# Four frequency groups of a spectral block: products summed on GpSimd and transposed by DMA, and the join's other TensorE work moved to other steps

## The chip, the cores and the metric

The kernel runs on one core of one Trainium2 chip. The metric is the device time of one launch in microseconds (us). A core has TensorE (PE; its weight loads are shown as PEld), VectorE (DVE), ScalarE (ACT), GpSimd (POOL) and SyncE (SP, which here issues nearly all DMAs). Each engine works through its own instructions in program order and waits on semaphores.

## The reference

One transformer block with adaptive layer norm, on x of 2048 x 640 (bf16): a global spectral filter (a 2-D real FFT over tokens and channels, a product with a complex weight, the inverse FFT), then a gated feed-forward of width 1728.

```python
mod = (_silu(c) @ w_mod).reshape(c.shape[0], 6, 1, -1)
sa, ca, ga, sb, cb, gb = (mod[:, i] for i in range(6))
h = _layernorm(x) * (1 + ca) + sa
X = jnp.fft.rfft2(h.astype(jnp.float32), axes=(-2, -1)) * (w_r + 1j * w_i)
x = x + ga * jnp.fft.irfft2(X, s=(S, D), axes=(-2, -1)).astype(jnp.bfloat16)
h = _layernorm(x) * (1 + cb) + sb
x = x + gb * ((_silu(h @ w_gate) * (h @ w_up)) @ w_down)
```

## The kernel before, in words

It is one long program in five stages. The order of each engine's instructions is the order of the Python calls; nothing is reordered afterwards.

1. **Forward transform** (to about 33 us): layer norm of x, a DFT over tokens and channels as matmuls, result in `A_sb`, for 81 of the channel frequencies l (the rest follow by symmetry).
2. **Join** (about 33 to 61 us; lines 515 to 812), where the change lies. The 81 frequencies are cut into 21 groups of mostly four (`groups`, `NG = 21`; group 4 holds l = 0 and 80, group 5 three). A loop over steps g = 0 to 21 works as a hand-written pipeline. For group g + 2, `stage_a`: `mix` (four PE matmuls, L581, out of transposed blocks `B2` that four DMA transposes and four PE transposes made) into one of two PSUM bank pairs, then `prod` (two DVE products with the weight table `Wt`, L605) into the SBUF tile `PPs[g]`, one of four slots, where the frequency index is the innermost. For group g, `stage_b`: eight PE matmuls with the identity (L613) that at once add the two halves of the complex product and transpose it, and an ACT copy to `Y2` (L616). For pairs of groups, some steps later, `stage_c`: PE matmuls with the inverse table (L643), and `evac`, an ACT copy of two banks (L652) to `Em` (l below 64) or `Er`.
   Into these steps other work is laid: the gate vector `ga_mod` (L713, steps 1 and 2), the weight table's mirrored columns `turn` (L381, ACT copies L387) and `wsum` (POOL, L424), a special path for frequency 0 over tokens (`sp_w`, `sp_gather`, `sp_mm`, `sp_ev`; steps 3, 5, 9, 11, 13), whose last step copies two rows to SBUF and has SP move them by DMA to partition 127 (L707, L708), and the modulation columns `mod_col` (L594). Already there, and unused, is `presum`: with a group in the set `PRE` (empty), POOL would add the halves and PE would only transpose.
   The pairs' `stage_c` comes at the step of their last group + 2.
3. **Inverse transform over channels** (about 61 to 80 us): 16 token tiles t; `s1em`, `s1er` (L729, L738), then L1266 and L1269, and a DVE sum with x (L1271). After t = 1 the second layer norm of the first two tiles runs; at t = 4 SP issues its DMA transpose (`ln2_tr`, L871), POOL scales the result (`ln2_mod`, L879), and at t = 15 PE begins the feed-forward with it (`gu13`, L1083).
4. **Feed-forward of the first two tiles** (L1095, L973) and 5. **of the other 14 tiles** (L996, L1125), PE without a pause to the end.

SP's queue in the join, in order: four DMA transposes `t2_dma` (L541), the tables `Htab` (L551) and `RI` (L552), two 800 KB pieces of `w_mod` (L553, L554; the second is used in step 20 only), the two rows of the special path (L707, L708, after ACT's copy L706), `B_w_down` (L815 to L819), `Wp13` (L822, L823), three loads of gate and up weights (L827), the transpose of stage 3 (L871), and the last two loads of up weights (L827). `presum` and its place in the loop are these lines:

```python
if 1 < g < NG - 2 and g + 2 in PRE:
    presum(g + 2)
...
for u, gs in enumerate(units):
    if gs[-1] + (1 if gs[0] >= NG - 2 else 2) == g:
        stage_c(u)
        evac(u)
```

Of the kernel before, what the change touches and what calls it, by code (L numbers as in the profile page):

```python
# [11 lines left out]
BF16 = mybir.dt.bfloat16  # L12
# [3 lines left out]
ALU = mybir.AluOpType  # L16

S, D, FF = 2048, 640, 1728
NT, P = 16, 128
# [147 lines left out]
def adaln_block_kernel(ctx, tc, A_x, A_w_r, A_w_i, B_x, B_w_gate, B_w_up, B_w_down, c, w_mod, out):  # L167
# [165 lines left out]
    if True:  # L333
# [41 lines left out]
        def turn(lo, i, b=3, eng=None):  # L375
            hi = lo + 16
            lo = max(lo, 1)
            n = hi - lo
            ps = psum[:, b, 0:32 * n].rearrange("p (a k c l) -> p a k c l", a=2, k=8, c=2)
            for a in range(2):  # L380
                nc.tensor.matmul(ps[:, a], lhsT=flipb[:], rhs=_rev(Wraw, 2568 * i + (161 - hi if a else lo), [[321, 8], [160, 2], [1, n]]),  # L381
                                 start=True, stop=True)
            if b < 4:
# [50 lines left out]
        def sp_w():  # L434
            tp = psum[0:81, 4, 192:256].bitcast(BF16).rearrange("p (v h a k) -> p v h a k", v=2, h=2, a=2)
# [98 lines left out]
    if True:  # L534
# [18 lines left out]
        nc.sync.dma_start(wm_r[:, :, 2, :], wm_m[:, :, 2, :])  # L553
        nc.sync.dma_start(wm_r[:, :, 3, :], wm_m[:, :, 3, :])  # L554
        Wd_sb = rA.cut(0, [NFC, D])
# [41 lines left out]
        def prod(g, xps, hl, v0=0, v1=3):  # L597
            ls = groups[g]
            n = len(ls)
            if g not in PPs:  # L600
                PPs[g] = rM.cut(1536 * (g % 4), [3, 2, NT, 2, n])
            xv = xps[:, :n, 0:192].rearrange("p i (v h k m) -> p v h k m i", v=3, h=2, k=NT)
            st = ls[1] - ls[0]
            in1 = _rev(Wt, (160 - ls[0] if hl else ls[0]) + WP * v0, [[WP, v1 - v0], [321, NT], [160, 2], [-st if hl else st, n]])
            nc.vector.tensor_tensor(PPs[g][:, v0:v1, hl], xv[:, v0:v1, hl], in1, ALU.mult)  # L605

        def stage_b(g, PP):
            n = len(groups[g])
            yps = banks((g + 1) % 2, 1, [4, 128])
            Q = Qs.pop(g, None)  # L610
            for ps in (1, 0) if Q is None else (0,):
                for i in range(n):
                    nc.tensor.matmul(yps[:, i, :], lhsT=_rev(PP if Q is None else Q, 64 * n * ps + i, [[n, 128]]), rhs=identb[:],  # L613
                                     start=(i == 0 and (ps == 1 or Q is not None)), stop=(ps == 0 and i == n - 1))
            Y2 = rY.cut(4096 if g == 4 else 1024 * (g % 4), [4, 128])
# [29 lines left out]
        def evac(u):  # L645
# [5 lines left out]
            else:  # L651
                (nc.vector.tensor_copy if g == NG - 6 else nc.scalar.copy)(  # L652
                    ep_views(l0 // 4 * 4, 8), banks(4 if g == NG - 4 else 6, 2, [8, 128])[0:127].rearrange("p i q -> p q i"))
# [8 lines left out]

        def gap(parts, i, w, b):
            return psum[0:parts, b + i // 2, 192 + 256 * (i % 2):192 + 256 * (i % 2) + w]

        def sp_mm(i, g):
            b = 2 + 2 * (g % 2)
            if i == 3:
# [22 lines left out]
        def sp_ev(i, g):  # L691
            b = 2 + 2 * (g % 2)
            if i == 3:
# [48 lines left out]

        PPs, Y2s, Qs = {}, {}, {}
        PRE = set()
        SPG = (9, 11, 13, 5)
        t2_pe(0)
# [11 lines left out]
        turn(32, 1, 7, act)  # L758
        wsum(32, 48, 8, nc.gpsimd)
        for rk in (0, 8):  # L760
# [3 lines left out]
        for g in range(NG + 1):  # L764
            if g == 9:
                nc.gpsimd.tensor_copy(sgnc[:], Kstab[:, 576:577])
            if g == 6:
                sp_gather()
            if 1 < g < NG - 2:
                if g in SPG:  # L770
                    sp_mm(SPG.index(g), g)
                if g == 3:
                    tp = sp_w()
                stage_a(g + 2)
                if g == 3:
                    sp_wc(tp)
                if g in SPG:
# [3 lines left out]
            if g in (4, 9):  # L781
                wsum(64, 80, 8 * (g // 9), nc.gpsimd)
            if g in (11, 12):
                h4 = slice(4 * (g - 11), 4 * (g - 11) + 4)
                nc.gpsimd.tensor_scalar(sgn_H[:, h4, 1], sgn_H[:, h4, 0], sgnc[:, 0:1], 1.0, ALU.mult, ALU.mult)
            if g == NG - 3:
                nc.vector.tensor_copy(modcols[:, 2, :], psum[:, 2, 192:197])
                nc.vector.tensor_scalar_add(one_p_cb[:], psum[:, 4, 192:197], 1.0)
            if g in (14, 16):
                i = (16 - g) // 2  # L790
# [7 lines left out]
            if g == 6:  # L798
# [605 lines left out]
```

## Time and profile before

| what | value |
|---|---|
| time, median of 3 runs | 249.57 us (247.81 to 250.02) |
| the profiled execution | 248.34 us, of which the span of its instructions is 246.3 us |
| busy over the span | PE 97%, PEld 76%, DVE 83%, ACT 69%, POOL 29% |
| granted TensorE clock | 1.00 |
| `stage_b` matmuls L613 | eight in 0.45 us |
| `prod` L605 (128 x 384) | mean 549 ns, one every 0.47 us back to back |
| ACT copy L616, ACT copy L652 | mean 598 ns, 1026 ns |
| DMA transpose of the first two tiles (L871) | issued at 70.39 us, landed 7.03 us later |

How to read it: times inside the execution count from the first instruction. A busy PE is near the bound only where it has no gaps; what a change in one stage is worth depends on which wait ends last there, and the chain of waits that ended last is the view for that. "Landing" of a DMA is the time from its issue until its semaphore says that all data are there.

### The profile page before, as it was taken

What the parts mean: (1) busy time and instruction counts of PE and PEld (TensorE: products, weight loads), DVE (VectorE), ACT (ScalarE), POOL (GpSimd) and SP (SyncE); (2) the same over time, 40 slices, a digit from 0 to 9 for tenths busy, and PEclk for the clock granted to TensorE, in tenths of its full rate; (3) what the DMA queues carried; (4) which work ended last, traced back from release to release, by engine and by line L of the source; (5) the groups of instructions that cost most, each with busy time, mean ns of one, the idle gap of its engine ahead of it and who ended that gap; (6) DMA issues with size and microseconds to landing.
All of it is one profiled execution on the core that took longest, in us unless ns stands there. A gap on an engine that the chain in (4) does not pass through costs nothing.

```text
span 246.3 us, 6008 instructions
## 1 busy us (share of the span) xinstructions
PE 239.1 (97%) x2262; PEld 187.8 (76%) x2262; DVE 203.4 (83%) x479; ACT 171.2 (69%) x343; POOL 70.9 (29%) x116
## 2 busy tenths in 40 slices
PE   8889999999999999999999999999999999999994
PEld 2678889999998887788887778887765666656773
DVE  4798777897499996989989968788998777789964
ACT  4789887998988797588864588765247777773220
POOL 4368896660424523002004400001422000004400
PEclk9999999999999999999999999999999999999999
DMA  6999979969999999500005110202411000000111
GB/s 204 381 339 290 342 179 179 253 234 293 289 374 266 194 266 190 123 3 1 3 0 106 59 53 3 53 0 43 86 38 53 0 1 3 0 0 4 53 53 53
DMA packets 44142, 31.19 MB, mean 127 GB/s; under 512 B 21873, under 2 KB 41810, under 8 KB 44114
## 3 DMA queue, kind: packets, MB, share of 16 engines
q1 hardware_dynamic: 42176, 26.15, 39.8%
q0 software_dynamic: 1376, 4.26, 7.5%
q10 hardware_dynamic: 562, 0.41, 0.6%
q8 instruction: 17, 0.28, 0.5%
q14 instruction: 11, 0.09, 0.1%
HBM read 23.49 MB, written 2.62 MB: 106 GB/s over the span
## 4 chain that ended last, share of the span: by engine, by line
PE 84%; DMA 5%; DVE 4%; POOL 2%; ACT 2%; issue 1%; ACTq 0%; DVEq 0%; POOLq 0%
PE psum L1125 36%; PE psum L996 19%; PE psum L1095 6%; PE psum L613 4%; PE psum L973 3%; DMA rW<-rL 3%; PE psum L581 3%; PE psum L404 2%; DMA rX<-in_A_x_dram 2%; PE psum L643 2%; PE psum L1083 2%; DVE bn6a L337 2%; PE psum L729 1%; ACT rE L407 1%; DVE rE L369 1%; POOL rW L879 1%
## 5 line engine op out<-in xcount | busy, mean ns | idle before, releaser
L1125 PEld LDWEIGHTS <-rW 128*128 128x128 bf16 (+1 forms) x429 | 41.9, 98 | 12.6
L1125 PE MATMUL psum<-rW 128*128 128x256 bf16 (+1 forms) x247 | 42.2, 287 | 0.0
L1022 POOL TENSOR_TENSOR rM<-rM,rL 128x320 f32<-128x320 f32 x6 | 5.5, 909 | 97.1 <-ACT rL L1021 97.1
L996 PEld LDWEIGHTS <-rE 128*128 128x128 f16 (+1 forms) x196 | 18.9, 97 | 8.0 <-DVE rE L950 0.3
L605 DVE TENSOR_TENSOR rM<-psum,rW 128x384 bf16<-128x384 f32 (+2 forms) x42 | 20.5, 543 | 4.0 <-PE psum L581 2.7
L996 PE MATMUL psum<-rE 128*128 128x320 f16 (+1 forms) x147 | 22.9, 299 | 0.0
L1163 ACT COPY rX<-psum 128x384 f32<-128x384 f32 (+2 forms) x27 | 14.0, 519 | 7.4 <-PE psum L1125 7.3
L1156 ACT COPY rH<-psum 128x384 f32<-128x384 f32 (+2 forms) x27 | 14.0, 517 | 7.2 <-PE psum L1125 6.5
L1125 PEld LDWEIGHTS <-rE 128*128 128x128 f16 x156 | 15.3, 98 | 4.7
L1160 DVE TENSOR_TENSOR rH<-psum,rM 128x512 bf16<-128x512 f32 (+1 forms) x24 | 15.0, 624 | 4.1 <-PE psum L1125 2.2
L1179 ACT ACTIVATE rL<-psum 128x384 bf16<-128x384 f32 (+2 forms) x27 | 14.4, 533 | 5.4 <-PE psum L1125 3.4
L1164 DVE TENSOR_TENSOR rX<-psum,rX 128x384 f32<-128x384 f32 (+2 forms) x27 | 16.3, 604 | 1.6 <-ACT rX L1163 1.4
L1150 ACT COPY rM<-psum 128x384 f32<-128x384 f32 (+2 forms) x27 | 13.9, 516 | 4.0 <-PE psum L1125 3.9
L1271 DVE SCALAR_TENSOR_TENSOR rM<-psum,rX 128x640 f32<-128x640 f32 x16 | 13.1, 821 | 3.9 <-ACT rL L733 2.4
L1125 PE MATMUL psum<-rW,rE 128*128 128x256 bf16 (+1 forms) x78 | 15.6, 290 | 0.0
L1125 PE MATMUL psum<-rE,rY 128*128 128x256 f16 (+1 forms) x78 | 15.6, 290 | 0.0
L1180 ACT ACTIVATE rL<-rX 128x384 bf16<-128x384 f32 (+2 forms) x27 | 15.1, 558 | 0.0
L337 DVE BATCH_NORM_STATS2 bn6a<-rX 128x6 f32<-128x320 bf16 x30 | 13.1, 480 | 2.4 <-DMA rX<-in_A_x_dram 2.4
L1095 PE MATMUL psum<-rW 128*128 128x256 bf16 x130 | 14.4, 273 | 0.0
L965 DVE TENSOR_TENSOR rA<-psum,rM 128x320 bf16<-128x320 f32 (+1 forms) x27 | 12.1, 472 | 2.4 <-PE psum L973 2.3
L424 POOL TENSOR_TENSOR rW<-rW 128x256 bf16<-128x256 bf16 x20 | 13.5, 704 | 1.4 <-DMA rW<-in_A_w_r_dram 0.7
L1095 PEld LDWEIGHTS <-rW 128*128 128x128 bf16 x130 | 12.7, 98 | 1.5
(231 smaller groups left out, 633.0 us busy)
## 6 DMA issues: line engine op xcount, KB each, us to landing
rM<-in_w_mod_dram SPq DMA_DIRECT2D x4, 800.0 KB, 8.1
out_dram<-rA SPq DMA_DIRECT2D x31, 80.0 KB, 1.6
rX<-in_A_x_dram SPq DMA_DIRECT2D x6, 320.0 KB, 6.3
rA<-in_B_w_down_dram SPq DMA_DIRECT2D x2, 960.0 KB, 6.3
rY<-in_B_w_gate_dram POOLq DMA_DIRECT2D x2, 832.0 KB, 7.8
rW<-in_B_w_gate_dram SPq DMA_DIRECT2D x1, 1440.0 KB, 10.0
rW<-in_A_w_i_dram SPq DMA_DIRECT2D x2, 642.0 KB, 11.1
rW<-in_A_w_r_dram SPq DMA_DIRECT2D x2, 642.0 KB, 10.5
```

What stands on the lines that cost most here:

```text
L337: nc.vector.bn_stats(bn6a[:, i % 2, k, :], x_sb[:, i, 320 * k:320 * k + 320])
L605: nc.vector.tensor_tensor(PPs[g][:, v0:v1, hl], xv[:, v0:v1, hl], in1, ALU.mult)
L996: nc.tensor.matmul(o, lhsT=lhs[rows(k), k], rhs=rhs[rows(k), k], start=start and k == ks[0], stop=stop and k == ks[-1], skip_group_check=True)
L1095: nc.tensor.matmul(gu[u], lhsT=Wgu[:, u, c5, ff * 128:(ff + 1) * 128], rhs=h2T[:, :, c5, :], start=(c5 == 0), stop=(c5 == NC5 - 1))
L1125: nc.tensor.matmul(o[:, f], lhsT=w, rhs=b, start=(start and f == 0 and i == 0), stop=(stop and f == len(groups[g]) - 1 and i == len(ops) - ...
L1150: nc.scalar.copy(c0, X)
L1156: nc.scalar.copy(c2, X)
L1160: nc.vector.tensor_tensor(c11, Z, c0, ALU.add)
L1163: nc.scalar.copy(c3, X)
L1164: nc.vector.tensor_tensor(c22, Y, c3, ALU.add)
L1179: nc.scalar.activation(g21, X, ACT.Silu, scale=-1.0)
L1180: nc.scalar.activation(g22, c22, ACT.Silu, scale=-1.0)
```

## The change

- Groups 7, 8, 11 and 12 are now in `PRE`. Their products are stored with the frequency outermost, POOL adds the halves (`presum`, 512 columns each, in steps 5, 6, 9, 10) into `Qd`, and after each second one SP issues a DMA transpose of 128 x 1024 into `Yd`, which `stage_c` uses directly. Their `stage_b` is gone: 32 PE matmuls with their weight loads, four ACT copies.
- `stage_c` of the pairs has a table of steps, `CAT`: (5,6) at step 7 instead of 8, (7,8) at 14 instead of 10, (9,10) at 11 instead of 12, (11,12) at 20 instead of 14, (17,18) at 19 instead of 20.
- `ga_mod` goes to steps 11 and 12, `turn(64)` to steps 7 and 8 (into the PSUM banks that `stage_b` leaves free), the special path to steps 5, 11, 13, 15 (its transposes `sp_w` to step 2), the columns `mod_col` from steps 16 to 18 to 7, 9, 14, 16, 18.
- The load of `w_mod`'s last piece goes from before the join to step 10, in SP's queue behind the second new transpose.
- Small moves: `sp_gather` from step 6 to 7, one `wsum` to step 2 and one from step 9 to 10; the evacuation that DVE does is now of pair (17,18).

```diff
-        nc.sync.dma_start(wm_r[:, :, 3, :], wm_m[:, :, 3, :])
...
-                    for c5 in {NG - 3: (0, 1), NG - 2: range(NC5), NG - 1: (2, 3, 4)}.get(g, ()):
-                        mod_col(psum[:, 2 + 2 * (g % 2), 192 + c5:193 + c5], wm_r[:, :, 1 + g % 2], c5)
+                    for c5 in {9: (0, 1, 2), 11: (3, 4), 16: (0, 1), 18: (2, 3), 20: (4,)}.get(g, ()):
+                        mod_col(psum[:, 2 + 2 * (g % 2), 192 + c5:193 + c5], wm_r[:, :, 2 - g % 2], c5)
...
-                PPs[g] = rM.cut(1536 * (g % 4), [3, 2, NT, 2, n])
+                PPs[g] = (rM.cut(1536 * (g % 4), [n, 3, 2, NT, 2]).rearrange("p l v h k m -> p v h k m l") if g in PRE else
+                          rM.cut(1536 * (g % 4), [3, 2, NT, 2, n]))
...
         def presum(g):
-            m = 128 * len(groups[g])
-            Qs[g] = rE.cut(21504 + 1024 * (g % 3), [m])
-            nc.gpsimd.tensor_tensor(Qs[g], _rev(PPs[g], 0, [[1, m]]), _rev(PPs[g], m // 2, [[1, m]]), ALU.add)
+            b, i = PRE.index(g) // 2, 4 * (PRE.index(g) % 2)
+            q = Qd[b][:, i:i + 4, :]
+            P3 = PPs.pop(g).rearrange("p v h k m l -> p l (v h k m)")
+            nc.gpsimd.tensor_tensor(q, P3[:, :, 0:128], P3[:, :, 64:192], ALU.add)
+            Y2s[g] = Yd[b][:, i:i + 4, :]
+            if i:
+                nc.sync.dma_start_transpose(Yd[b], Qd[b].rearrange("p l j -> p (l j)"))
...
-        PRE = set()
-        SPG = (9, 11, 13, 5)
+        PRE = (7, 8, 11, 12)
+        Qd = [rE.cut(21504 + 2048 * (i % 2), [8, 128]) for i in range(len(PRE) // 2)]
+        Yd = [rE.cut(26144 + 2048 * i, [8, 128]) for i in range(len(PRE) // 2)]
+        CAT = (3, 5, 7, 14, 11, 20, 16, 18, 19, 20, 21)
+        SPG, GAG, TUG = (11, 13, 15, 5), (11, 12), (7, 8)
...
-            if 1 < g < NG - 2 and g + 2 in PRE:
+            if g + 2 in PRE:
                 presum(g + 2)
...
+            if g == 10:
+                nc.sync.dma_start(wm_r[:, :, 3, :], wm_m[:, :, 3, :])
...
-            if g < NG:
+            if g < NG and g not in PRE:
                 Y2s[g] = stage_b(g, PPs.pop(g))
+            if g == SPG[0]:
+                sp_mm(0, g)
+                sp_ev(0, g)
...
-            if 0 < g < 3:
-                ga_mod(320 * (2 - g), 8 - g)
-            if g == 6:
-                turn(64, 0, 6, act)
-                turn(64, 1, 7, act)
+            if g in GAG:
+                ga_mod(320 * GAG.index(g), 0)
+            for i in range(2):
+                if TUG[i] == g:
+                    turn(64, i, (g + 1) % 2, act)
             for u, gs in enumerate(units):
-                if gs[-1] + (1 if gs[0] >= NG - 2 else 2) == g:
+                if CAT[u] == g:
                     stage_c(u)
                     evac(u)
```

More of the change, by code (lines that the diff above doesn't have):

```diff
@@ L434, in sp_w @@
         def sp_w():
-            tp = psum[0:81, 4, 192:256].bitcast(BF16).rearrange("p (v h a k) -> p v h a k", v=2, h=2, a=2)
+            tp = psum[0:81, 2, 192:256].bitcast(BF16).rearrange("p (v h a k) -> p v h a k", v=2, h=2, a=2)
             for v in range(2):
@@ L609, in stage_b @@
             yps = banks((g + 1) % 2, 1, [4, 128])
-            Q = Qs.pop(g, None)
-            for ps in (1, 0) if Q is None else (0,):
+            for ps in (1, 0):
                 for i in range(n):
-                    nc.tensor.matmul(yps[:, i, :], lhsT=_rev(PP if Q is None else Q, 64 * n * ps + i, [[n, 128]]), rhs=identb[:],
-                                     start=(i == 0 and (ps == 1 or Q is not None)), stop=(ps == 0 and i == n - 1))
+                    nc.tensor.matmul(yps[:, i, :], lhsT=_rev(PP, 64 * n * ps + i, [[n, 128]]), rhs=identb[:],
+                                     start=(i == 0 and ps == 1), stop=(ps == 0 and i == n - 1))
             Y2 = rY.cut(4096 if g == 4 else 1024 * (g % 4), [4, 128])
@@ L651, in evac @@
             else:
-                (nc.vector.tensor_copy if g == NG - 6 else nc.scalar.copy)(
+                (nc.vector.tensor_copy if g in (17,) else nc.scalar.copy)(
                     ep_views(l0 // 4 * 4, 8), banks(4 if g == NG - 4 else 6, 2, [8, 128])[0:127].rearrange("p i q -> p q i"))
@@ L663, in gap @@
         def gap(parts, i, w, b):
+            if b < 2:
+                return psum[0:parts, b, 320 + 64 * i:320 + 64 * i + w]
             return psum[0:parts, b + i // 2, 192 + 256 * (i % 2):192 + 256 * (i % 2) + w]
         def sp_mm(i, g):
-            b = 2 + 2 * (g % 2)
+            b = 2 + 2 * (g % 2) if i else 1
             if i == 3:
@@ L691, in sp_ev @@
         def sp_ev(i, g):
-            b = 2 + 2 * (g % 2)
+            b = 2 + 2 * (g % 2) if i else 1
             if i == 3:
@@ L766, in adaln_block_kernel @@
                 nc.gpsimd.tensor_copy(sgnc[:], Kstab[:, 576:577])
-            if g == 6:
+            if g == 7:
                 sp_gather()
             if 1 < g < NG - 2:
-                if g in SPG:
+                if g in SPG[1:]:
                     sp_mm(SPG.index(g), g)
-                if g == 3:
+                if g == 2:
                     tp = sp_w()
                 stage_a(g + 2)
+                if g == 2:
+                    wsum(32, 48, 8, nc.gpsimd)
                 if g == 3:
                     sp_wc(tp)
-                if g in SPG:
+                if g in SPG[1:]:
                     sp_ev(SPG.index(g), g)
-            if 1 < g < NG - 2 and g + 2 in PRE:
+            if g + 2 in PRE:
                 presum(g + 2)
-            if g in (4, 9):
-                wsum(64, 80, 8 * (g // 9), nc.gpsimd)
+            if g in (4, 10):
+                wsum(64, 80, 8 * (4, 10).index(g), nc.gpsimd)
+            if g == 10:
+                nc.sync.dma_start(wm_r[:, :, 3, :], wm_m[:, :, 3, :])
             if g in (11, 12):
@@ L785, in adaln_block_kernel @@
                 nc.gpsimd.tensor_scalar(sgn_H[:, h4, 1], sgn_H[:, h4, 0], sgnc[:, 0:1], 1.0, ALU.mult, ALU.mult)
+            if g == 9:
+                nc.vector.tensor_copy(modcols[:, 2, :], psum[:, 4, 192:197])
             if g == NG - 3:
[L787 to L788 removed]
+                nc.vector.tensor_scalar_add(one_p_cb[:], psum[:, 2, 192:197], 1.0)
             if g in (14, 16):
[L790 removed]
+                i = 1 - (14, 16).index(g)
                 nc.gpsimd.tensor_tensor(RI[:, i], RI[:, i], ga_bc[:], ALU.mult)
[L792 removed]
+            if g < NG and g not in PRE:
                 Y2s[g] = stage_b(g, PPs.pop(g))
+            if g == SPG[0]:
+                sp_mm(0, g)
+                sp_ev(0, g)
             if g == 0:
                 stage_a(3)
[L796 to L800 removed]
+            if g in GAG:
[3 more added lines that the diff above has]
+                    turn(64, i, (g + 1) % 2, act)
             for u, gs in enumerate(units):
[L802 removed]
+                if CAT[u] == g:
                     stage_c(u)
```

5 lines of the change are left out of this document (2 added, 3 removed).

## The prediction

> **What bounds the kernel now.** I read the page's chain first (PE holds 84% of it), then the chain of waits between 39 and 81 us in order of time. The join is PE almost without a gap, then comes one piece that is not PE: a DMA transpose of 7.03 us, POOL's scaling, and only then PE goes on.
>
> ```profile
> 43.34 0.93 ACT rE L652
> 44.27 0.04 issue
> 44.31 0.64 PE psum L381 x4
> ...
> 48.22 0.45 PE psum L613 x8
> 48.67 0.45 PE psum L643 x8
> ...
> 70.39 7.03 DMA rW<-rL
> 77.42 0.11 issue
> 77.53 2.17 POOL rW L879 x4
> 79.69 0.04 issue
> 79.74 0.38 PE psum L1083 x2
> ```
>
> The timeline of PE shows how little that chain leaves: PE came to this matmul 0.25 us before POOL was done. So stage 3 has two bounds that end together, PE's own work and the arrival of the transpose, and a shorter join pays only if both come earlier.
>
> ```profile
> 79.74 0.38 PE L1083 MATMUL psum<-rW,Wp 128*128 128x256 bf16 x2 [0.25 <-POOL rW L879]
> ```
>
> Why does that transpose take 7 us? The timeline of SP (issue time, how long the issue held the queue) and the DMA share by stretch (last two columns) tell it:
>
> ```profile
> 45.39 0.42 SPq L553 DMA_DIRECT2D rM<-in_w_mod_dram  x1
> 45.86 0.52 SPq L554 DMA_DIRECT2D rM<-in_w_mod_dram  x1
> 53.36 0.54 SPq L707 DMA_DIRECT2D rE<-rE  x1
> 53.95 0.61 SPq L708 DMA_DIRECT2D rE<-rE  x1
> 54.66 1.12 SPq L815 DMA_DIRECT2D rA<-in_B_w_down_dram  x2
> ...
> 64.81 0.92 SPq L827 DMA_DIRECT2D rW<-in_B_w_up_dram  x1
> 70.39 1.44 SPq L871 DMA_TRANSPOSE rW<-rL  x1
> ```
>
> ```profile
> 52.00:54.00 2.00, 1.98 (x33) 1.86 (x31) 1.85 (x4) 2.00 (x6) 1.25 (x1) 1.00 0.53 186
> 54.00:56.00 2.00, 2.00 (x45) 2.00 (x43) 1.76 (x4) 2.00 (x4) 0.00 (x0) 1.00 0.24 32
> 56.00:58.00 2.00, 2.00 (x58) 2.00 (x55) 1.21 (x3) 1.65 (x3) 0.00 (x0) 1.00 0.82 223
> 58.00:60.00 2.00, 2.00 (x39) 2.00 (x38) 1.90 (x5) 1.13 (x4) 0.00 (x0) 1.00 1.06 385
> ```
>
> The DMA engines idle from about 53 to 57 us, because SP stands at L707 for ACT's copy of the special path (6.9 us, SP's waits). From 57 to 78 us they are full (share about 1): some 5 MB of weights, issued from 54.66 on, lie ahead of the transpose. So the time at which SP gets past L707 sets when the weights start, and with it when the transpose lands. That step moves from 13 to 15.
>
> **The change, part by part.**
>
> *Removed from PE:* four `stage_b` of 0.45 us, 1.78 us, and the 0.32 us for which `turn` waited for ACT's L652. ACT loses four copies of 0.6 us; it is off the path. `ga_mod` (2 x 0.68), `turn`, `sp_mm` and the columns only change place. 64 rows of matmul and weight load less stand in the instruction order of the changed kernel, so the change does what it says.
>
> *POOL* gains four sums of 512. L661 (16 elements) took 0.22 us and L791 (640) 1.41, so 1.9 ns an element, 1.2 us each. POOL ended its join work at 53.2 us, and what it makes last (RI) is read at 62.97; 4.7 us more end at about 58. Hidden; without that cover it would be 4.7 us. SP's queue is held by the two transposes until POOL has the sums; behind the second stand the 800 KB load, the rows and the weights, but the sums are there by 51.5, before the rows' own wait ends.
>
> *DVE:* the 8 half products of these groups write single bf16 elements 384 B apart, where they wrote dense runs. The trace has no such write of that length. From below: no cost (writes in runs of four elements, L419, take 1.04 ns an element as dense ones do). The nearest row is group 4, whose two frequencies are read 160 B apart: 192 elements took 524 ns, more than the 447 to 458 for 288 elements of group 5; one came every 0.44 us, 1.9 ns an element beside 1.04. Applied to 384 elements: 0.33 us a half, 2.7 us in all. From above: L393, 40 elements written 160 B apart, took 294 ns, where 41 dense ones (L695) took 191: 2.5 ns more an element, 0.95 us a half, 7.6 us. I take 2.7.
> [...]
>
> *When PE reaches step 14's `stage_c`, the first use of a transposed block:* in this execution step 14's `stage_c` began at 53.10. By PE's work: minus 1.78, minus 0.32, minus one `stage_c` (0.45) and one `sp_mm` (0.20) that now come later, plus 35 column matmuls that now come earlier (25 took 0.60, so 0.84): 51.2, and about 0.4 for two new waits on ACT (the special path's bank in step 11, `ga_mod`'s in step 13): 51.6. By DVE: group 14's products ended at 51.7; minus idle that goes (1.0 for POOL's L762, 0.9 for PE), plus 2.7, is 52.5, then `mix` with its columns 0.57 and `stage_b` 0.45: 53.5.
>
> *When the block is there:* its sums are made by 47, but the transpose stands in SP's queue behind `Htab`, RI and the 800 KB of L553, which landed 7.3 us after 45.39, at 52.7. 256 KB at the 288 GB/s at which the earlier transposes ran are 0.9 us, and their semaphores came some 0.4 us after the data: 54.0. From below: without L554's 800 KB behind it, 1.67 MB from 45.7 on at 350 GB/s are through at 50.5, so 51.9. I take 53.6, near the observed landing of the same load.
>
> So the three times are 51.6, 53.5 and 53.6; step 14's `stage_c` starts at 53.6. PE saved 1.8 us and stands them out there.
>
> *Past L707:* `stage_c` 0.45, 0.2 until ACT starts, L652 0.95, the special path's copies 0.3: SP is free at 55.55 instead of 53.36, 2.2 us later. The weights are issued at 56.85. The load of 800 KB behind the second transpose (0.9 us, then 2.3 us) is through by 56.5 and falls into the idle stretch: no cost. If the DMA engines are full until the transpose, it lands 2.2 us later, at 79.6. From below: the stretch 74 to 76 us moved 141 GB/s where its neighbours moved 303 to 353, so about 1.2 us could be made good. I take 2.0: POOL is done at 81.7, and PE goes on 2.0 us later than before.
>
> *The end of the join:* by DVE and PE from 53.6 on, `s1em` starts at about 61.9 (61.4 before), since step 20 now has (11,12)'s `stage_c` and ACT's copy in front of it. PE would be at L1083 at 80.0. Hidden behind 81.7. From there PE runs without pauses to the end.
>
> *Sum:* 248.34 + 2.0 = 250.3 us for an execution like the profiled one. With both ends of the block's landing and of the recovery: 248.34 + 0.5 to + 2.6. The median of the runs shown is 1.2 above the profiled execution and their mean with it 0.6; I forecast 250.9 for a median, and 249.5 to 251.6 for this case.
>
> **The rivals.**
>
> 1. *Same time (no stall).* The block lands before PE is there and scattered writes cost nothing: `stage_c` at 51.6, rows at 53.6, weights 0.2 later than before. The shorter join then waits at L1083: 248.3 to 248.9, about 249.1 for a median. For it: the emptier queue. Against it: the observed 52.7.
> 2. *Faster.* As rival 1, and the transpose of stage 3 isn't held by the weights' start but by work that moves with PE (POOL's own 832 KB load, issued at 68.41). Then PE's 1.8 us less 0.3 come through: 246.8, about 247.4 for a median. It decides if SP passes L707 before 53.4. Against it: full DMA engines since 57 us.
> 3. *Slower by scattered writes.* At 0.95 us a half DVE needs 7.6 us more, of which 2.7 were hidden: `stage_c` of step 14 at about 58.4, all behind it 4.8 later: 255. It decides once a half costs over about 0.35 us. For it: L393; against it: that L393's second instruction started only 0.12 us after the first.
> 4. *Slower by a late block.* The second of the earlier transposes landed 4.2 us after the first (37.5, 41.7), the others 1.7 to 1.8 apart. Such a hitch of 2.4 us in the new one puts its landing at 56 and the end at 252.7, 253.3 for a median.
>
> **How the numbers follow.** Forecast 0.46, rival 1 0.16, rival 2 0.08, rival 3 0.18, rival 4 0.12. A measurement of this kernel can tell about 1%, 2.5 us, from no change. Faster by over 1%: rival 2 in part, 0.06. Slower by over 1%: rivals 3 and 4 and the upper third of the forecast, 0.43. Within 1%: 0.51. The range leaves out 2 in 10: 248.2 (below it rival 2 and a little of rival 1) to 255.0 (above it half of rival 3).
>
> **What would show it.** In the changed kernel's profile: a wait of PE at L643 in step 14 of 1 to 2 us, released by the DMA `rE<-rE`, or by DVE shortly before; mean of L605 in its 128x3x32x4 form near 0.88 us (0.55: no penalty; 1.5: rival 3); the rows' issue at 55 to 56 us; the landing of stage 3's transpose near 79.6 and a wait of PE for POOL at L1083 of 1 to 2 us. I am wrong if the rows are issued before 54 us, or if L1083 does not wait although they are late.

## The result and the profile after

| | before | changed |
|---|---|---|
| time, median of 6 runs on one chip | 248.13 us (247.67 to 250.02) | 260.51 us (260.34 to 263.48) |
| ratio, 95% interval | | 1.051 (1.046 to 1.056) |
| the profiled execution | 248.34 us (span 246.3) | 263.48 us (span 261.7, the longest of the six) |
| first `mix` to `s1em` (the join) | 33.61 to 61.22 us: 27.61 | 34.31 to 70.64 us: 36.33 |
| `s1em` until PE goes on at `gu13` | to 79.74: 18.52 | to 92.72: 22.08 |

The change made the kernel slower by 12.4 us in the medians, far outside the forecast range. Line numbers of the changed kernel are a little higher: L580 is `mix`, L605 still `prod`, L612 `stage_b`, L622 POOL's sum and L625 its transpose, L646 `stage_c`, L712 the rows, L830 `B_w_down`, L886 the transpose of stage 3, L1098 `gu13`.

Of the 15.4 us between the two spans, 0.7 are there before the join, 8.7 are the join, 3.6 stage 3, and 2.4 come behind it. The timeline of VectorE shows where the join lost them (start, length, line, number of instructions in the row):

```profile
41.55 4.66 DVE L605 TENSOR_TENSOR rM<-psum,rW 128x384 bf16<-128x384 f32 x4 [0.58 <-PE psum L580]
46.21 5.44 DVE L605 TENSOR_TENSOR rM<-psum,rW 128x384 bf16<-128x384 f32 x6
52.02 3.62 DVE L605 TENSOR_TENSOR rM<-psum,rW 128x384 bf16<-128x384 f32 x2 [0.38 <-PE psum L580]
55.30 4.63 DVE L605 TENSOR_TENSOR rM<-psum,rW 128x384 bf16<-128x384 f32 x4
60.23 2.93 DVE L605 TENSOR_TENSOR rM<-psum,rW 128x384 bf16<-128x384 f32 x6
```

Six ordinary halves take 2.93 us together (last row). The two halves at 52.02 are both of a group in `PRE`; they take 3.62. Over all 38 halves of this shape, scattered and ordinary together, the mean went from 549 to 867 ns:

```profile
L605 DVE TENSOR_TENSOR rM<-psum,rW 128x384 bf16<-128x384 f32 x38 | 28.6, 867 | 2.3 <-PE psum L580 1.9 <-ACT rY L615 0.3
```

38 x (867 - 549) ns are 12 us; spread over the 8 scattered halves that would be 1.5 us each, and counted from one start to the next it is 1.70 instead of 0.465, so 1.24 us more. In the table by stretch (busy time of PE, PEld, DVE, ACT, POOL, then granted clock, DMA share, GB/s), DVE is full in 44 to 48 and 56 to 60 us and PE about half idle. After the first of these stretches and after the wait at 88 to 90 us the clock is 0.50; after 56 to 60 it stays at 1.00:

```profile
44.00:48.00 4.00, 1.79 (x28) 1.50 (x26) 4.00 (x6) 0.98 (x3) 1.15 (x1) 0.83 0.88 226
48.00:52.00 4.00, 3.05 (x31) 2.65 (x30) 3.60 (x6) 2.25 (x5) 2.12 (x7) 0.50 0.84 289
56.00:60.00 4.00, 2.31 (x27) 1.85 (x25) 4.00 (x6) 1.44 (x2) 1.71 (x2) 1.00 0.00 0
60.00:64.00 4.00, 3.93 (x77) 3.63 (x75) 3.67 (x11) 2.14 (x6) 4.00 (x6) 1.00 0.56 86
88.00:90.00 2.00, 0.51 (x6) 0.27 (x4) 2.00 (x6) 0.18 (x1) 0.00 (x0) 1.00 0.66 164
92.00:94.00 2.00, 1.67 (x9) 1.01 (x8) 0.00 (x0) 0.38 (x1) 2.00 (x4) 0.50 1.04 346
```

SP's timeline shows what the late products do to the queue. Its first row covers both new transposes: they hold SP to 61.57, the second until POOL has its sum at 60.32; the load, the rows and the weights stand behind it. Before, the rows went out at 53.36 and the weights at 54.66:

```profile
51.06 10.52 SPq L625 DMA_TRANSPOSE rE<-rE  x2
61.63 0.57 SPq L793 DMA_DIRECT2D rM<-in_w_mod_dram  x1
64.92 0.55 SPq L712 DMA_DIRECT2D rE<-rE  x1
...
66.17 1.98 SPq L830 DMA_DIRECT2D rA<-in_B_w_down_dram  x2
```

In the chain of waits the transpose of stage 3 then takes 10.58 us where it took 7.03:

```profile
79.83 10.58 DMA rW<-rL
...
90.52 0.68 POOL rW L894 x2
...
92.72 0.59 PE psum L1098 x2
```

Measured from the start of `s1em`, the weights were issued 6.56 us ahead of it before and 4.47 ahead now: 2.1 us, near the forecast's 2.2. The clock is 0.50 from 91.02 to 97.84 us; of this PE works 5.1 us, from 92.72 on, which is up to 2.6 us lost and accounts for the 2.4 us behind the wait.

### The profile page after: what moved, and what is told of

It is laid out like the page before. It is cut to its first block, busy times and chain, and to the rows that moved or that the text cites. A ratio compares the mean times of both kernels' runs of the same rounds, so it can differ in the third digit from the quotient of the medians.

```text
span 261.7 us, 5941 instructions
## 1 busy us (share of the span) xinstructions
PE 243.2 (93%) x2230; PEld 189.3 (72%) x2230; DVE 213.4 (82%) x479; ACT 169.4 (65%) x339; POOL 75.5 (29%) x120
## 4 chain that ended last, share of the span: by engine, by line
PE 74%; DVE 8%; DMA 8%; ACT 3%; issue 3%; POOL 2%; ACTq 0%; DVEq 0%; SPq 0%; POOLq 0%
PE psum L1140 34%; PE psum L1011 18%; PE psum L1110 6%; DVE rM L605 4%; DMA rW<-rL 4%; PE psum L988 3%; PE psum L404 2%; PE psum L580 2%; DMA rX<-in_A_x_dram 2%; DMA rW<-in_B_w_gate_dram 2%; PE psum L1098 2%; DVE bn6a L337 2%; ACT rE L407 1%; ACT rY L615 1%; PE psum L734 1%
## 5 line engine op out<-in xcount | busy, mean ns | idle before, releaser
L605 DVE TENSOR_TENSOR rM<-psum,rW 128x384 bf16<-128x384 f32 (+2 forms) x42 | 30.3, 831 | 2.5 <-PE psum L580 2.2
L1110 PE MATMUL psum<-rW 128*128 128x256 bf16 x130 | 16.2, 292 | 0.0
L1110 PEld LDWEIGHTS <-rW 128*128 128x128 bf16 x130 | 13.6, 105 | 2.4
L580 PE MATMUL psum<-Ktab,rL 128*128 128x192 bf16 x47 | 7.5, 280 | 7.3 <-DVE rM L605 2.6
```

The source lines that it names most:

```text
L1110: nc.tensor.matmul(gu[u], lhsT=Wgu[:, u, c5, ff * 128:(ff + 1) * 128], rhs=h2T[:, :, c5, :], start=(c5 == 0), stop=(c5 == NC5 - 1))
```

## The experiments

Theory A: VectorE's scattered writes cost about 1.25 us a half, 10 us in all, and the late weights and the low clock follow. Rivals: B, SP's queue and the moved steps; C, VectorE slowed by POOL beside it.

### Dense writes in the changed kernel: e1_dense

```diff
-                PPs[g] = (rM.cut(1536 * (g % 4), [n, 3, 2, NT, 2]).rearrange("p l v h k m -> p v h k m l") if g in PRE else
-                          rM.cut(1536 * (g % 4), [3, 2, NT, 2, n]))
+                PPs[g] = rM.cut(1536 * (g % 4), [3, 2, NT, 2, n])
```

> The changed kernel, but VectorE stores the products of groups 7, 8, 11 and 12 in dense runs of four, as the kernel before does; POOL's sums read them with a step of four elements (8 bytes) instead. The sums, the turn by DMA, the queue order and the moved steps stay. Theory A (the loss is VectorE's scattered writes, 1.25 us more for each of 8 halves, about 10 us, of which 8.6 appear as a longer join, and the rest follows from the late weights and the lower clock): the halves fall back to 0.55 us, stage_c of step 14 starts near 53, the rows of the special path are issued near 55.5, and the time is 249.5 to 252 us. Theory B (the loss comes from SP's queue: the second transpose holds the rows and the weights, and the 800 KB load stands behind it): the rows stay late, at 60 us or more, and the time stays at 255 us or above. Theory C (VectorE is slowed by POOL, whose sums run beside it): the halves stay above 1 us, and the time stays near 260 us.

Measured: 253.96 us beside 249.52, ratio 1.017 (1.011 to 1.023), so two thirds of the loss are gone. The halves are back at the old price, though POOL still runs beside them (against C), the rows go out at 57.46 (against B, which had 60 or more), and POOL pays 0.35 us a sum for reading with a step:

```profile
L604 DVE TENSOR_TENSOR rM<-psum,rW 128x384 bf16<-128x384 f32 x38 | 18.9, 551 | 5.6 <-PE psum L580 5.2 <-ACT rY L614 0.3
...
L621 POOL TENSOR_TENSOR rE<-rM 128x512 bf16<-128x512 bf16 x4 | 5.9, 1505 | 0.7 <-PE psum L580 0.7
```

The upper end of theory A's range was 2 us too low. PE's timeline shows a wait that I had not listed: the first columns of the second `w_mod` piece, moved to the mix of group 16, meet their load (L553, landed at 52.9 us), and behind the wait the clock halves:

```profile
52.91 0.40 PE L593 MATMUL psum<-sc_col,rM 128*128 128x1 bf16 x10 [1.40 <-DMA rM<-in_w_mod_dram]
```

```profile
52.00:54.00 2.00, 1.09 (x21) 1.09 (x22) 0.31 (x1) 0.75 (x3) 2.00 (x3) 0.91 1.03 218
54.00:56.00 2.00, 2.00 (x22) 1.96 (x21) 0.71 (x2) 1.41 (x2) 2.00 (x3) 0.50 0.96 234
```

### Scattered writes alone in the kernel before: e2_scatter_alone

```diff
+        SCAT = (7, 8, 11, 12)
...
-                PPs[g] = rM.cut(1536 * (g % 4), [3, 2, NT, 2, n])
+                PPs[g] = (rM.cut(1536 * (g % 4), [n, 3, 2, NT, 2]).rearrange("p l v h k m -> p v h k m l") if g in SCAT else
+                          rM.cut(1536 * (g % 4), [3, 2, NT, 2, n]))
...
+                    nc.tensor.matmul(yps[:, i, :], lhsT=_rev(PP, 64 * ps + 192 * i, [[1, 128]]) if g in SCAT else
```

> The kernel before, in its old order and with nothing turned by DMA or summed by POOL; only the products of groups 7, 8, 11 and 12 are stored as the change stores them, single elements 384 bytes apart, and PE reads them back accordingly (columns now next to each other). Theory A: each of the 8 halves takes 1.8 us or more instead of 0.55, 10 us in all; VectorE was idle for 4.3 of the 27.6 us of the join (23.3 busy), so the join grows by 5.7 to 8.6 us, the weights start as much later, and the time is 254 to 260 us. Theory B or C (the loss is that of the queue, the moves or POOL's sums): 248 to 250 us, or at most 1 to 3 us more for slower writes.

Measured: 260.07 us beside 249.52, ratio 1.045 (1.038 to 1.052). With nothing else of the change, these writes cost 10.5 us, the upper end of theory A's range. The profiled execution, the longest of the four, has a join of 40.4 us, more than I had expected: the clock is 0.50 from 50.5 to 57.3 us and from 60.8 to 67.6, which the expectation had left out. B and C are not needed for the size of the loss.

```profile
L606 DVE TENSOR_TENSOR rM<-psum,rW 128x384 bf16<-128x384 f32 x38 | 29.0, 864 | 6.0 <-PE psum L581 5.6
```

### The price by itself: m1_write_steps

> A kernel by itself, which leaves out the whole computation and writes zeros to the output; only the durations of its instructions are read. VectorE multiplies 384 elements a partition (PSUM by SBUF, bf16 out) four times for each way of writing: dense (L63), the change's single elements 384 bytes apart (L65), steps of 4, 8, 16, 32 and 192 bytes (L67 to L75), pairs and runs of four 384 bytes apart (L77, L79), and dense writes with reads 32 bytes apart (L81); then copies by VectorE and ScalarE, dense and scattered (L83 to L93), and POOL's sum of 512 elements, dense and read with a step of 8 bytes (L95, L97). Theory A (the step of the write alone costs): L65 1.5 to 2.0 us beside 0.45 to 0.55 for L63, with runs of four about as dense ones. By group 4's row and by L393, on which the prediction built, L65 would take 0.8 to 1.4 us. Theory C (contention with POOL or PE in the kernel): L65 about as L63, below 0.7 us, since nothing else runs. Where between 4 and 384 bytes the cost sets in is open: if each element pays by itself, steps of 32 and 192 bytes cost as 384 does, and pairs half as much.

Measured, with nothing else running (groups of the trace: line, ..., busy, mean ns of one):

```profile
L75 DVE TENSOR_TENSOR dst<-psum,src 128x384 bf16<-128x384 f32 x4 | 8.3, 2077 | 0.2
L71 DVE TENSOR_TENSOR dst<-psum,src 128x384 bf16<-128x384 f32 x4 | 7.5, 1870 | 0.1
L65 DVE TENSOR_TENSOR dst<-psum,src 128x384 bf16<-128x384 f32 x4 | 7.5, 1868 | 0.1
...
L69 DVE TENSOR_TENSOR dst<-psum,src 128x384 bf16<-128x384 f32 x4 | 4.0, 1012 | 0.1
L81 DVE TENSOR_TENSOR dst<-psum,src 128x384 bf16<-128x384 f32 x4 | 3.4, 839 | 0.1
L67 DVE TENSOR_TENSOR dst<-psum,src 128x384 bf16<-128x384 f32 x4 | 2.4, 588 | 0.1
L77 DVE TENSOR_TENSOR dst<-psum,src 128x384 bf16<-128x384 f32 x4 | 2.2, 558 | 0.1
...
L63 DVE TENSOR_TENSOR dst<-psum,src 128x384 bf16<-128x384 f32 x4 | 2.2, 542 | 0.1
```

Dense (L63) takes 542 ns, the change's layout (L65) 1868: 3.45 ns more an element. A step of 4 bytes (L67) costs 46 ns in all, 8 bytes (L69) 1.9 times the dense time, and 16 bytes (L71) already as much as 384. Pairs 384 bytes apart (L77) take 558 ns, nearly as little as dense: from 16 bytes on (1758 to 2077 ns at steps of 16, 32, 192 and 384) it is the single element that costs, and not the distance. Reading with a step of 32 bytes (L81) costs only 0.77 ns an element. ScalarE pays as much (L93, scattered, 1872 ns beside 478 for L91).

### Late rows alone: e4_rows_late

```diff
-        SPG = (9, 11, 13, 5)
+        SPG = (11, 13, 15, 5)
```

> The kernel before, with the three special-path steps two steps later (11, 13, 15 in place of 9, 11, 13), and nothing else: the rows at L707, and the weights behind them on SP, come about two steps, 2.4 to 2.8 us, later. Theory A (the start of the weights sets when stage 3's transpose lands, as the prediction has it): the transpose lands 2.0 to 2.8 us later than at 77.6 us, PE waits for POOL at L1083, and the time is 250.3 to 251.5 us. Rival (the transpose is held by something else, or the delay is made good in the DMA engines): within 0.5 us of before, 247.7 to 248.8 us.

Measured: 251.08 us beside 249.52, ratio 1.007 (1.0035 to 1.011). The weights came 1.6 us later (two steps were less than I expected), the transpose landed at 78.6 instead of 77.4, and PE went on at 81.26 instead of 79.74, though `s1em` had begun 0.6 us earlier. The forecast's claim that L707 sets the end holds. That the time fell into the expected range is in part luck: the delay was smaller than expected, and eight of the twelve runs had a mean clock of 0.986 to 0.993, which the expectation did not contain and the profiled execution (249.36 us, 0.998) does not show.

```profile
69.81 8.79 DMA rW<-rL
...
78.71 2.51 POOL rW L879 x4
...
81.26 0.38 PE psum L1083 x2
```

### What is left without scattered writes: e5 to e9, e11, e12

The next runs were to take away the rest of e1_dense's loss. Three of them failed in the same way:

```diff
+            if g == 10:
+                for h in range(2):
+                    nc.sync.dma_start(Wd_sb[:, HK * h:HK * h + 6, :],
...
-                nc.sync.dma_start(Er[127:128].rearrange("p v q c j -> p (v q c j)"), Osp[:, 64:80])
+                nc.scalar.dma_start(Er[127:128].rearrange("p v q c j -> p (v q c j)"), Osp[:, 64:80])
```

These are lines of e5; the other loads of `Wd_sb` (the tile that `B_w_down` goes to) and of `Wp13` and the first row move likewise, and e6, on the kernel before, has `g == 4`.

> The changed kernel with dense products (as e1_dense), and besides the Wd and Wp13 loads issued on SP at step 10, right behind the 800 KB load, instead of behind the rows of the special path; the rows go out on ACT's queue. e1_dense still lost 4.4 us of median; in its trace the rows were issued at 57.46 us (before 53.36), the weights at 58.95 (54.66), stage 3's transpose landed at 81.95 (77.4), and PE went on at 84.27 (79.74). Theory A (that chain, rows to weights to transpose, is what is left): with the weights freed from the rows they start near 53, the transpose lands at or before 78, PE goes on at 80 or earlier, and the time is 249 to 251 us, 3 to 5 us below e1_dense. Rival D (what is left is PE's own stall in the join, the 1.4 us for the columns of the w_mod piece that lands at 52.9, and the lower clock behind it; the weights only come late with it): the time falls by less than 1.5 us, to 252.5 to 254.

> The kernel before, with the Wd and Wp13 loads issued on SP at step 4 and the rows of the special path on ACT's queue; nothing else. Theory A says stage 3's transpose then lands earlier than at 77.4 us, by up to 5 us, but PE's own work now ends at 79.5 (it waited only 0.25 us at L1083), so the gain is at most 0.3 us and the time 247.8 to 249.6 (before 249.5 median). Rival: PE gains more than 1 us because transfers in the join or behind it were slowing it: 248.5 or less by interval; or the rows on ACT's queue and the early 2 MB delay the w_mod piece and the join: 250.5 or more.

> As e5_dense_early_weights, and besides the first columns of the w_mod piece that PE waited for in e1_dense (1.4 us at 51.5 to 52.9) come two mixes later (18 and 20 in place of 16, 18, 20), and the load of that piece is issued behind the first transposed block instead of ahead of it, so that the block is there earlier than 53.8 us. Theory D (PE's stall in step 14 and the clock that falls to half behind it make the rest): no clock of 0.5 in the join, stage_c of step 14 starts at 52 to 53, and the time is 1 to 3 us below e5_dense_early_weights: 246.5 to 249. If the forecast's first sum was right (PE's saving of 2.1 us comes through once nothing is late), it ends 0.5 to 2 us below before. Rival: the stall only moves to the next late thing (DVE's products, ACT's copies), and the time stays within 0.7 us of e5_dense_early_weights.

Measured beside 248.72: e5 260.30 us, ratio 1.047 (1.043 to 1.050); e6 259.86, 1.045 (1.041 to 1.048); e7 259.39, 1.042 (1.040 to 1.045). All three expectations missed, for a reason that has nothing to do with them. In the traces the second row's transfer is issued only when a `B_w_down` load from SP's queue has landed (e6: landed at 64.74, issued at 64.76), and ACT, on whose queue it was, stood until then; that the transfer had been given that load's semaphore is inferred from this wait. The waits of e6 name the load (in total, times, longest, us):

```profile
ACT rY L617 <- DMA rA<-in_B_w_down_dram: 10.7, 1, 10.7
```

Only e7's first half can be read: with its columns two mixes later and their load behind the first new block, PE ran from 44 us to 55.96 without a pause above 0.2 us. Next, that edit alone on e1_dense:

```diff
-        nc.sync.dma_start(wm_r[:, :, 2, :], wm_m[:, :, 2, :])
...
-                    for c5 in {9: (0, 1, 2), 11: (3, 4), 16: (0, 1), 18: (2, 3), 20: (4,)}.get(g, ()):
+                    for c5 in {9: (0, 1, 2), 11: (3, 4), 18: (0, 1, 2), 20: (3, 4)}.get(g, ()):
...
+            if g == 7:
+                nc.sync.dma_start(wm_r[:, :, 2, :], wm_m[:, :, 2, :])
```

> e1_dense with the first columns of the w_mod piece two mixes later and that piece's load behind the first transposed block; the weights stay behind the rows on SP, as in the change. (In e7_cols_later_too these two edits worked, PE ran without a pause to 55.96 us and stage_c of step 14 began at 52.3; then ACT stood 10.4 us for a semaphore of a Wd load, since the second row's transfer on its queue had been given that load's semaphore. So e5, e6 and e7 say nothing on the early weights.) Theory A+D: no clock of 0.5 in the join; rows issued at 54.7 to 55.5 us, weights at 56 to 56.8 (before 54.66), stage 3's transpose lands at 79 to 79.8, PE goes on at 81.2 to 82, and the time is 249.5 to 251.5 us, 2.5 to 4.5 below e1_dense, 1 to 2.5 above before: what the prediction's sum gives without scattered writes. Rival: the clock falls again while PE waits at 80 to 82, and it stays at 252 to 253.

Measured: 251.95 us beside 248.83, ratio 1.011 (1.006 to 1.016), 0.5 us above the expected range. The chain is the expected one: rows issued at 54.99, weights at 56.22, transpose landed at 79.28, PE on at 81.62.

```profile
70.09 9.19 DMA rW<-rL
...
79.39 2.18 POOL rW L894 x4
81.62 0.38 PE psum L1098 x2
```

PE had been ready at 78.8 and then took POOL's pieces as they came. After that wait the rival came too, one short spell of half clock:

```profile
82.00:83.00 1.00, 1.00 (x10) 0.82 (x9) 0.42 (x1) 0.38 (x1) 1.00 (x2) 0.74 0.86 283
83.00:84.00 1.00, 1.00 (x7) 0.69 (x6) 0.82 (x3) 0.41 (x2) 1.00 (x2) 0.50 0.67 87
84.00:85.00 1.00, 1.00 (x6) 0.75 (x5) 0.27 (x1) 0.69 (x2) 1.00 (x2) 0.50 0.91 143
```

Now early weights, with both rows on POOL's queue (e9, and the same kernel once more as e11; the other loads of `Wd_sb` and the first row move likewise):

```diff
+            if g == 10:
+                for h in range(2):
+                    nc.sync.dma_start(Wd_sb[:, HK * h:HK * h + 6, :],
...
-                nc.sync.dma_start(Er[127:128].rearrange("p v q c j -> p (v q c j)"), Osp[:, 64:80])
+                nc.gpsimd.dma_start(Er[127:128].rearrange("p v q c j -> p (v q c j)"), Osp[:, 64:80])
```

> e8_dense_cols_later, and the Wd loads on SP at step 10, behind the 800 KB load and ahead of the rows; the rows go out on POOL's queue, whose transfers have semaphores of their own, so that no engine stands behind a Wd load. Theory A: the weights start near 53 us, the transpose lands before 78, PE comes to the scaled weights about when POOL has made them (79 to 80), and the time is 247 to 249.5 us, 1.5 to 3 us below e8_dense_cols_later. Rival 1: the rows, whose transfer now stands behind 2 MB of Wd, come too late for stage 3 (needed at 61.5 to 62), and the time does not fall. Rival 2: the DMA engines have no time to spare, the transpose lands as late as in e8, and the time is the same within 0.7 us.

> The kernel of e9_dense_wd_early once more, for a profile: the one that was taken ran at a clock of 0.75 throughout (307 us, where the other 11 runs took 248.9 to 251.3). Its median of 250.4 us was 1.5 below e8_dense_cols_later as theory A had it, yet 1.6 above before, with less work on PE. Theory A: the transpose lands before 78 us and PE does not wait for it by more than 0.5 us; what is lost then lies elsewhere, in the join (PE's saved 2.1 us stood out there, by DVE or ACT) or behind 82 us. Rival (the weights still set the end): the transpose lands at 79 us or later and PE waits 1 us or more, with the clock at 0.5 behind the wait. Time 249 to 251 us.

Measured: e9 250.40 us beside 248.83, ratio 1.006 (1.003 to 1.008); e11 249.15 beside 250.05, 0.999 (0.995 to 1.003). The late transpose no longer holds PE (it landed at 78.71, and PE came later still), and rival 1 of e9 took its place. No wait of 1.4 us or more for a `B_w_down` load stands in the waits of e9 and e11. `s1em` waits for the rows: issued at 55.19 and 56.02, with `B_w_down` already in the DMA engines, they landed at 62.22 and 62.82, and the clock was 0.50 from 63.0 to 66.4 us.

```profile
62.31 0.38 PE L733 MATMUL psum<-rH,rE 128*128 128x128 bf16 x4 [2.13 <-issue]
```

Last, only half of `B_w_down` ahead of the rows, these on SP again:

```diff
+                nc.sync.dma_start(Wd_sb[:, 0:6, :], B_w_down[0:768, :].rearrange("(fc fp) d -> fp fc d", fp=P))
```

> e8_dense_cols_later with only the first half of Wd (0.98 MB) on SP at step 10, behind the 800 KB load and ahead of the rows; the rows stay on SP, the other half behind them. In e11_wd_early_again the join ended at 60.2 us (before 61.4), then PE stood 2.1 us for the rows, whose transfer lay behind all of Wd, and the clock fell to 0.5 from about 62.5 to 66 us; stage 3's transpose no longer held PE. Theory A+D: with half as much ahead of them the rows land near 58, s1em starts at 60.2 to 60.6, the transpose lands before 78, PE has no wait above 0.5 us, and the time is 246 to 248 us, 1 to 3 us below before: the change's saving on PE comes through at last. Rival 1: the transpose is late again (79 us or more) and the time is 249.5 to 251. Rival 2: something else holds stage 3 (DVE, ACT), and the time is within 0.5 us of before.

Measured: 249.45 us beside 249.39, ratio 1.002 (0.9985 to 1.005). The expectation was 1 to 3 us too low, and rival 2's time came true: the rows were issued from 56.44 on and the second still landed at 63.70, just behind the half of `B_w_down` (63.27). PE waited 1.2 us before `s1em`, to 63.55 (ACT's last copy was done at 62.97, so the first row is the likely end of the wait), and 0.6 us more at `gu13`.

### The same load orders without the change: e10 and e13

> The kernel before, with the Wd loads on SP at step 4 and the rows on POOL's queue; nothing else. Theory A: the transpose lands before 77.4 us, but PE's own work ends at 79.5, so the gain is at most 0.3 us: 247.9 to 249.3, or the same as before within the interval. Rival 1: it gains more than 1 us (below 247.7), and then the transpose held before back by more than the trace says. Rival 2: the Wd loads, now ahead of it in the DMA engines, delay the rows, and it loses 1 us or more.

> The control: the kernel before with the first half of Wd on SP at step 4, rows and the rest as they were. PE's own work sets the end there (it waited 0.25 us at L1083), so theory A says a gain of at most 0.3 us, as e10_before_wd_early had it (ratio 0.997): 247.8 to 249.5. If it gains as much as e12_dense_half_wd_early, the gain there is the load's and not the change's.

Measured: e10 248.14 us beside 248.83, ratio 0.997 (0.994 to 0.9996); e13 247.80 beside 249.39, 0.995 (0.991 to 0.999). The kernel before gains 0.3 to 0.5% from an earlier load, somewhat more than theory A allowed for e13. e13 is the best version found, by a difference near what can be measured; the change contributes nothing to it: beside the same runs of before, e12, which has the change and half of the same load early, gains nothing.

### The clock: m2_clock

> A kernel by itself, which leaves out the whole computation and writes zeros to the output; only PE's clock is read. PE runs bursts of 70 matmuls of 512 columns (some 15 us), with a pause between two bursts of about 1.0, 1.5, 2.0, 2.5, 3.0, 3.0, 3.5, 3.5, 4.5 and 6.0 us (a VectorE write that the next burst waits for); then six stretches in which short bursts (4, 4, 2, 1, 2, 2 matmuls) alternate with pauses of 0.4 or 0.8 us, 8 or 3 times. In the changed kernel the granted clock fell to 0.5 for 6.83 us twice, after 4 us in which PE was busy 1.79 us; in e1_dense after 4 us with 2.5 us busy and again after a wait of some 2 us. Theory (PE's own idleness lowers the clock): pauses of 3.5 us and more are each followed by a stretch of 0.5, those of 1.0 us by none, and some pause between 1.5 and 3 us sets the limit, perhaps by chance of its place; the stretches at about half duty show it too. Rival (the drop comes from power or from other engines' load, not from PE's pauses): no drop after pauses of 2 to 3 us. [...]

The pauses came out longer than planned. Each row below covers a stretch (the clock is the third number from the end): behind a pause of 2.29 us, behind one of 3.53 us, then bursts of about 1.04 us with pauses of 0.80, and bursts of 1.04 to 1.89 us with pauses of 1.80:

```profile
53.00:57.00 4.00, 3.84 (x18) 1.76 (x19) 0.10 (x1) 0.00 (x0) 1.00 0.01 4
...
71.90:75.40 3.50, 3.42 (x10) 1.34 (x11) 0.02 (x1) 0.00 (x0) 0.60 0.00 0
```

```profile
295.00:309.00 14.00, 8.36 (x34) 2.67 (x35) 3.87 (x7) 0.00 (x0) 1.00 0.00 0
326.00:351.00 25.00, 12.43 (x29) 2.93 (x28) 9.43 (x7) 0.00 (x0) 0.55 0.00 0
```

All nine pauses of 3.53 us and more were followed by a stretch at 0.50, the one of 2.29 us was not, and none lay between. So in this kernel PE's own idleness halved its clock; nothing else ran here but the VectorE writes that make the pauses. A burst of 70 matmuls took 15.28 us behind the pause of 2.29 and 16.97 behind that of 3.53: 1.7 us lost, about 3.4 us at half speed.

Within each trace the clock changes only at times that lie whole multiples of 3.41 us apart (in the changed kernel at 46.64, 53.47, 91.02 and 97.84, so 2, 11 and 2 times 3.41 us). A stretch of 3.41 us on this grid is called a window here. A window need not be wholly idle to be followed by half clock. Here are the windows of the waits of 1.2 to 1.4 us in e1_dense and e8, each followed by a window at 0.50, and then the two into which the same kind of wait falls in e4, where the clock stayed at 1.00 (PE's busy time is the second number):

```profile
50.21:53.63 3.42, 1.93 (x35) 1.60 (x34) 1.50 (x4) 1.33 (x5) 3.42 (x5) 1.00 1.27 234
...
79.06:82.47 3.41, 1.66 (x12) 1.13 (x13) 2.37 (x8) 0.98 (x2) 3.08 (x6) 1.00 1.08 355
...
75.77:79.18 3.41, 2.72 (x37) 2.38 (x35) 3.17 (x9) 2.73 (x6) 0.47 (x1) 1.00 0.92 210
79.18:82.59 3.41, 2.13 (x17) 1.45 (x17) 1.73 (x7) 0.42 (x2) 3.41 (x6) 1.00 0.93 308
```

Divided into such windows (the last of each left out), the 14 traces in which the clock changes say how much work is enough. Of the windows at 1.00, all 25 with PE busy for 45% or less were followed by one at 0.50; of the ten between 46 and 57%, two were (those of e8 and e1_dense above); of the 831 busier ones, none. Back to 1.00 it went only behind a window with PE busy for 80% or more. So the same kind of wait cost half clock where it fell into one window (e1_dense, e8) and nothing where two shared it (e4). PE's busy time is modelled, so these bounds are rough, and what decides between 46 and 57% stays open.

## Why the prediction was wrong

1. *What bounds the kernel:* right. e4 moves L707 alone: the weights come 1.6 us later, `gu13` goes on 1.5 us later.
2. *Removed from PE:* little of the 2.1 us reaches the end of the join. Without scattered writes and the columns' wait (e8) the join takes 27.02 us instead of 27.61: PE is busy for 25.90 us in it instead of 27.22, so 1.3 us less, and half of that goes into a wait that the forecast did not list. A `mix` at 40.58 stands 0.64 us for VectorE's L445, as in the changed kernel (0.65) and in e1_dense (0.63). L445 copies the transposes of `sp_w` out of PSUM. The change moves them from bank 4 to bank 2, which is also a bank of this `mix`; that this is why it waits is likely, but was not tried alone.
3. *POOL's sums:* 1.15 us each, forecast 1.2. "The sums are there by 51.5" was wrong: the second pair came at 60.3, because its products did, and SP stood in the two transposes to 61.6. With dense writes SP was through it at 52.65.
4. *VectorE's scattered writes:* **this is the step that failed.** I took 0.33 us a half and 0.95 as the upper end; it is 1.24 from start to start in the kernel and 1.33 by itself, about 10 us for the eight instead of 2.7. Group 4's row was no price for it: it holds scattered reads (1.9 - 1.04, so 0.86 ns an element; m1 has 0.77 for reads), and I applied it to writes (3.45). No run shows the 2.7 us for writes; taking them instead of no cost was my estimate. L393 was the right kind, but one row of forty elements, 2.5 ns more each, is no upper end: m1 has up to 4.0 (192 bytes). I chose the row that the count resembled, and not the row of the same access. The sign that I named, a mean of 0.88 us, would have misled: the trace does not part the scattered halves from the others, and the 867 ns are the mean of all 38; the scattered ones took 1.8 to 2.1 us.
5. *The block in step 14:* 53.6 us forecast; in e1_dense it landed at 53.8. Missed was that the columns moved to mix 16 wait for a load that lands at 52.9.
6. *Past L707 to the end:* rows 55.55, weights 56.85, landing 79.6, PE 2.0 us later; e8 shows 54.99, 56.22, 79.28 and 1.9. Without scattered writes and the columns' wait the sum of 250.3 is close: e8's two runs at clock 1.00 took 249.82 and 251.16 us. Its median of 251.95 holds spells of half clock, which the sum does not have.
7. *The clock:* not in the sum at all, and no reason given. It is part of the loss behind PE's longer waits, 2.4 us behind stage 3 in the changed kernel.
8. *The rivals:* rival 3 had the mechanism, at 0.18. With 1.24 us in its sum the delay is 8 x 1.24 - 2.7 = 7.2 us instead of 4.8, and its 255 becomes 257.4; with the clock's 2.4 it is 259.8. That this comes near the median of 260.5 is chance: it is a sum for an execution like the profiled one, which took 263.48. Counted from the start of the join PE went on at `gu13` 12.3 us later (8.7 and 3.6), where this sum has 9.2; the half clock inside the join, from 46.64 to 53.47 us, is part of the rest. What of stage 3's other 1.5 us of delay is the DMA engines' (nearly still from 88 to 89 us, share 0.20 and 0.08) was not tried.

## What to carry to other kernels

A layout that makes another engine's access easy has to be paid where it is written: look for single elements in the innermost dimension of a write, and keep at least two neighbours together (m1: 1868 ns for single elements 384 bytes apart, 558 for pairs, 542 dense). Bound an unknown price by a row with the same kind of access (write or read, single or in runs), and let the upper end grow until such a row stops it. When TensorE will wait in a new place, add to the wait what the clock may take afterwards (in m2 1.7 us for about 3.4 us at half clock).

## What the runs showed of the hardware

- Single bf16 elements written 16 or more bytes apart cost VectorE 3.2 to 4.0 ns more each than dense ones (m1: 1758 to 2077 ns beside 542), and ScalarE 3.6 (384 bytes apart: 1872 beside 478); pairs cost next to nothing (558 ns beside 542).
- In these traces the clock of TensorE changes only on a grid of 3.41 us. Each of the 25 windows of that length at 1.00 with it busy for 45% or less was followed by 3.41 us or more at clock 0.50, none of the 831 with more than 57% was (14 traces). Such spells also come outside the changed stages: in the trace of e12 one lies at 9.13 to 12.54 us. One spell of 3.41 us lowers the mean clock of a run by about 0.007 (3.41 x 0.5 of e12's span of 248.8 us), and in the runs beside e8 the kernel before took 249.9 to 250.6 us at mean clocks of 0.990 to 0.993, where most runs at 1.00 took 247.8 to 249.1; where in those runs the spell lay is not on record.
- On one queue a small transfer landed only behind the large one ahead of it. The special path's rows (16 and 4 KB) landed at 59.11 and 59.27 us in e13, behind a load of 0.98 MB that landed at 58.94; in e12 the second, issued at 57.03, landed at 63.70 behind the same load (63.27). On another queue they were late too, but did not wait for all of it: in e10, on POOL's queue, they landed at 61.33 and 62.16, 6.8 us after their issue, and a part of `B_w_down` issued 6.7 us before the first landed at 63.17.
- A DMA issued from ACT stopped ACT for 10.25 us in e5, 10.7 in e6 and 10.43 in e7, until a `B_w_down` load from SP's queue had landed; that the two share a semaphore is inferred from this wait.
